# Polysketch attention and a multiplicative FFN on one core: a new global order of all steps behind the first batch's queries

## The chip, the cores and the metric

The kernel runs on one core of a Trainium2 chip. A core has five engines that run their own instruction streams side by side and wait for each other through semaphores: TensorE (PE, matrix products, with its weight loads shown apart as PEld), VectorE (DVE), ScalarE (ACT), GpSimd (POOL), and SyncE (SP), which here issues DMA transfers. Data lies in HBM, in SBUF (on-chip memory) and in PSUM (where matrix products land; eight banks).

The metric is the device time of one execution in microseconds (us). The kernel before has a median of 249.38 us over 3 runs (249.37 to 249.53).

## The reference

Four batches of four heads attend over 1088 positions of 32 dimensions; both queries and keys are turned into products of two 8-wide sketches, so no softmax and no score matrix is needed. The result, 4352 tokens of 128, goes through a gated feed-forward network (FFN) without a nonlinearity.

```python
def phi(x):
    a = np.einsum('rd,bhsd->bhsr', S1, x)      # r = 8
    b = np.einsum('rd,bhsd->bhsr', S2, x)
    return np.einsum('bhsi,bhsj->bhsij', a, b).reshape(*x.shape[:-1], r * r)
q_p, k_p = (phi(q), phi(k))
kv = np.einsum('bhsf,bhsd->bhfd', k_p, v)
z = np.sum(k_p, axis=2)
num = np.einsum('bhsf,bhfd->bhsd', q_p, kv)
den = np.einsum('bhsf,bhf->bhs', q_p, z)[..., None] + 1e-06
x = (num / den).transpose(0, 2, 1, 3).reshape(4352, 128)
a = x @ w1                                      # 128 x 1024
b = x @ w2
h = a * b @ w3                                  # 1024 x 1024
out = h @ w_out                                 # 1024 x 128
```

q, k and v are float32; the four weight matrices arrive as float64.

## The kernel before

All work is cut into named steps, a few instructions each. One long text, ORDER, lists every step once, in one global order. The kernel issues the steps in that order and chains each of the five engines' instructions to the one before it on the same engine, so ORDER fixes the sequence on every engine; what runs beside what follows from the waits. The compiler does not reorder anything.

```python
for name in ORDER.split():
    n = len(traced)
    steps.pop(name)()
```

Other tables at the top of the file belong to that order:

- SLOTS gives, for each kind of buffer, the buffer number of each allocation in the order in which they come. Kind b is the eight PSUM banks, raw the three landing buffers of the weights, x the three landing buffers that k, v and q share, and k_g, q_m, l, m and s are working buffers in SBUF. A step that takes over a buffer waits until its last readers are done.
- WARM[i] is the number of zero products in step warm{i} (line 255). They multiply a zero array and are read by nobody.
- POOL names the steps that run on GpSimd; without the name they run on VectorE. CPV names the copies that run on VectorE; without the name they run on ScalarE.
- Bulk loads on SP wait until the fourth load before them has landed (UNDER_WAY = 4). SP, too, goes strictly by ORDER.

The steps are named after what they work on. The prediction uses these:

- **s.** and **c.**: constants and sketch matrices. s.AR and the like belong to the preparation of the sketches.
- **w0 to w10**: the weights, float64 words made into float32. load (SP, lines 430, 433, 440), c and m (ScalarE, lines 263, 462, 484), j (VectorE, 466, 495), a0 and a1 (GpSimd, 470, 501). w0 and w1 belong to the matrices w1 and w2, number 2 is w_out, 3 to 10 are the rows of w3.
- **f0 to f7**: the fold of w3 and w_out into one matrix w3o: t is a transpose on VectorE (line 528), m eight products (534), o a copy (538). The FFN so needs no 1024 × 1024 product for the tokens.
- **k0 to k3**: the keys of a batch. load, zero (GpSimd clears the padding), max and lead and rest (the keys split into a leading and a remaining part, lines 214 and 651), gram (Gram products of the two, 659), G, T and N (small error-compensated sketch steps), ab, abt and kp (the features of the keys, 677), kv (769, 776), kvc, kqt and kq (the matrix that is multiplied by the queries' features).
- **q0, q1, q2, q3, q4, q6, qr**: queries (q4 and q6 are the last two whole batches, qr the rest tokens). tr, max, l2, l1, rm prepare; A0, C0 and C1 are the sketch products (1365, 1374); At, Ct, sm, st, sh, sl, sc make an error-compensated sketch (sl is line 1417); al, p01, p2, p12, dn, de, rc the denominator (1426 to 1454); bs, na to nn scale it (1459 to 1490); phi0 and phi1 the features (1509); pT0 and pT1 transpose them (1517); x multiplies them by kq (1527); xT0 to xT3 copy the result out of PSUM (1540, four copies each). After the queries' x come the tokens of the FFN.
- **g0 to g3**: the FFN of 512 tokens at a time, in eight slices of d_ff. For slice i, ia is x @ w1 (line 1799, a pair of products), ic its copy out of PSUM (1804), ib is x @ w2 (1809, a pair), im the elementwise product (1815), io the product by w3o (1835, a pair); oT transposes the output (1842), st stores it.
- **h4 and h6**: the FFN of the last two batches, 1024 tokens each, as a seven-product scheme after Strassen: a and b products of half arrays (1673), copies (1680), sums and elementwise products T and m (1685 to 1742), P products of half arrays (1759), k1 to k9 (1767 to 1785) and oT. **gr** is the FFN of the rest tokens (o at 1824).

Two queries matter most below. The chain for q4 and q6 runs sketch (TensorE), some thirty small steps on VectorE, ScalarE and GpSimd, phi, pT, then x on TensorE; between A0 and x TensorE works on g steps and folds.

Of the kernel before, what the change touches and what calls it, by code (L numbers as in the profile page):

```python
# [41 lines left out]
    "raw": "012012021020121",
    "s": "012345672403167520431760243517241",
    "x": "012012010221",
}

WARM = [27, 2, 3, 4, 4, 4, 1, 2, 1, 1, 2, 2, 1, 1]
# [18 lines left out]
    g0.1c g0.3c g2.1c g2.5c g2.6c g3.4c h4.0ad h4.0ae h4.0bd h4.1ac h4.2ad h4.k1 h6.2bd h6.3ae  # L66
    k0.kT1 k1.kvc k2.kT1 k2.kq k3.kT0 k3.kT1 k3.kq q0.xc0 q0.xc1
# [23 lines left out]
w2.load g0.6b g0.1a q1.pt1 k2.lead0 k2.rest0 q1.pc0 q1.pc1 q2.l2 q2.l1 q3.l1 g0.1b q1.x g0.5m q1.xT g0.3c g0.1c g0.1m  # L91
w9.m k1.Nr k2.gram0 k2.gram1 k2.gram2 k2.gram3 k2.gram4 k1.Nb k2.kT0 q3.rm q2.A0 q2.rm k1.kp0 k2.ab k2.abt q2.C0 q2.C1
g1.1a g1.1c v1.loadr k2.Gm q2.At q2.sm k2.Gt q2.Ct g1.5a w9.c k3.zero q2.st q3.A0 k2.Ga q3.C0 q3.C1 q3.Ct q2.sh k2.Gb
k3.load g1.7a v.s g1.7b g1.2a v1.load g1.7c q2.sl q2.sc q2.p01 q2.al q2.p2 k2.Gc q3.At g0.0b k1.kp1 q3.sm q3.st k1.kv0
q3.sh k2.T0 k1.kv2 k1.kv3 k1.kv1 k2.T1 k1.kvr k1.kvc kr1.kp g1.2c k2.Ta q2.p12 q2.dn q2.de k2.Tb g0.0m q2.rc g0.6m
q3.sl q3.sc q3.p01 w9.j g1.7m q1.restT q2.bs g1.6a g1.6c w2.c v2.zero q2.phi0 g1.2b k3.loadr g1.3a g1.3c g1.0a g1.5b
g1.3b k1.kqt warm12 w6.c w6.m g0.3b k1.kq g1.5c g1.4a k3.max g1.4c w5.load g1.1b v2.loadr kh3.load k0.Nr q2.load g1.3m
g1.5m g1.2m g1.0c q2.pT0 warm13 g1.0b k2.Tc q2.x g0.3m w9.a1 w5.m q2.xT0 k3.kT0 k2.N0 k2.N1 w5.c q3.al q3.p2 q3.p12
q3.dn w6.j g1.0m q3.de w7.load w2.m g1.4b w7.m w7.c w3.load w10.load w4.load v2.load w2.j k2.Na g1.4m k2.Nb q3.rc
k3.kT1 k3.lead0 q2.restT q3.bs g0.2b g2.6a g2.3a g2.1a g2.5a g2.4a g2.2a w5.j g1.1m g0.2m q3.phi0 k2.Nr g2.2b g2.0a  # L100
g2.3c g2.2c g2.4b g2.5c w3.c g1.6b k3.rest0 w9.a0 g2.4c w2.a0 g2.1c w2.a1 q4.tr k3.gram0 w6.a0 w5.a1 f6.t g2.2m
k3.gram1 k3.gram2 k3.gram3 k3.gram4 q3.pT0 f6.m g2.6b g2.6c g2.0c k3.Gm v.t g2.1b k3.Gt k3.Ga k3.Gb w7.j g2.4m q4.max
g2.7a g2.3b g1.6m q4.l2 w3.m k3.Gc w7.a0 g2.0b f6.o g2.3m w5.a0 w6.a1 v3.zero g2.1m q3.x q4.l1 k3.T0 k3.T1 g2.6m w3.j
g2.7c q4.rm g2.5b g2.5m q3.xT0 q3.load g2.7b g3.0a v3.load w8.load v3.loadr k3.Ta w4.m g3.0c g3.0b g3.0m g3.3a g3.1b
g3.1a g3.3c k3.Tb w3.a0 g3.1c g2.0m k2.kp1 q6.tr k3.Tc g2.7m w7.a1 f4.t g3.6a q3.restT g3.6c q4.A0 w3.a1 q6.max k3.ab
k3.N0 k3.abt k2.kp0 q4.C0 q4.C1 k3.N1 f4.m k3.kp1 g3.6b f0.t f3.t f4.o k3.kp0 f0.m q4.At q6.l2 g3.6m k2.kv0 k2.kv3
g3.1m w4.c w4.j k3.kv0 k3.kv1 k3.kv3 k3.kv2 k3.kvr q4.Ct q4.sm q6.l1 qr.max k3.kvc k2.kv1 k2.kv2 k2.kvr k2.kvc f3.m
w8.c f0.o f3.o w4.a1 w4.a0 g3.7a g3.7c g3.4b g2.0o k3.Na q4.st f1.t qr.l2 q6.rm q4.sh w10.m qr.l1 q4.sl q4.sc g3.5a
g3.4a g3.3b f1.m f1.o w10.c g3.4c g3.4m qr.rm k3.Nb q4.p01 w8.m q4.al k3.Nr k3.kqt g2.4o q6.A0 q6.C0 f2.t g3.3m q4.p2
v.3 q6.C1 k3.kq q6.At w8.j w8.a1 q6.Ct g2.6o g3.0o g3.4o qr.A0 qr.C0 qr.C1 qr.Ct q6.sm w10.j q6.st q6.sh q4.p12 w8.a0  # L110
g3.5b q6.sl w10.a1 q6.sc q4.dn qr.At g3.5c q4.de f5.t q4.rc g1.0o g1.1o q4.na q4.bs q4.nb f2.m q4.nm q4.nr qr.sm q6.al
q6.p01 q6.p2 g0.0o g0.1o q6.p12 f2.o g0.2o g0.6o k2.kqt g0.3o q4.ne g3.5m q4.nn q6.dn k2.kq f5.m f5.o g3.7b g3.2b
g1.6o g0.5o g0.4o w10.a0 qr.st f7.t f7.m g3.2a q4.phi0 q4.phi1 qr.sh qr.sl qr.sc f7.o q4.pT0 g3.2c q4.pT1 g2.5o g0.7o
# [36 lines left out]
def make_steps(ctx, tc, q, k, v, S1, S2, moe_w1, moe_w2, moe_w3, moe_w_out, out):  # L150
# [1784 lines left out]
```

## Time and profile before

| | before |
|---|---|
| median of 3 runs | 249.38 us (249.37 to 249.53) |
| the profiled execution | 248.89 us |
| its span on the core | 246.9 us |
| granted TensorE clock | 1.00 |
| read from HBM, written | 19.40 MB, 2.23 MB |

The span runs from the first to the last instruction that the profile shows. Busy time is given by engine; a row such as "L1835 PE MATMUL ps_o<-ab,w3o" names the line of the kernel, the engine, the operation, and what is written from what. Timeline rows begin with start and duration in us. The list of waits gives, for an engine, what it waited for: us in total, how often, the longest. "PE" in that list is time in which no product ran; "PEld" is the weight loads' own queue, whose waits are mostly hidden under running products. The chain of waits is followed back from the last instruction and here read in order of time.

### The profile page before, as it was taken

The numbers are of one execution on the slowest core, as the hardware profiler recorded it, in microseconds if no ns is written. First come the engines' busy times: TensorE is split into PE (matmuls) and PEld (weight loads), VectorE is DVE, ScalarE is ACT, GpSimd is POOL, SyncE is SP. The second block draws the span as 40 slices with busy tenths as digits, with TensorE's granted clock in tenths as the row PEclk, the third lists the DMA queues.
The fourth block names the chain that finished last, engine by engine and source line by source line (L and its number), as shares of the span: only waits on it lengthen the run. The fifth ranks groups of instructions, "written<-read, shape, count | busy, mean of one in ns | idle before, by whom it ended". The sixth has DMA issues, their size and how long they took to land.

```text
span 246.9 us, 6753 instructions
## 1 busy us (share of the span) xinstructions
PE 238.4 (97%) x2726; PEld 133.7 (54%) x2726; DVE 212.2 (86%) x426; ACT 121.8 (49%) x246; POOL 154.4 (63%) x198
## 2 busy tenths in 40 slices
PE   8999999999999999999999988999999999999994
PEld 6887464554445556856666434447653344463373
DVE  2787989988999889889899888588999699799892
ACT  3888965557865754674000195663562046430010
POOL 4475575608479489725579456998991927972111
PEclk9999999999999999999999999999999999999999
DMA  7969678275879776000000000340000004000034
GB/s 202 267 167 324 173 204 185 92 229 135 244 177 230 183 230 142 3 4 0 3 0 0 3 1 3 54 73 4 0 0 0 3 11 74 1 0 3 0 53 96
DMA packets 31934, 22.06 MB, mean 89 GB/s; under 512 B 21280, under 2 KB 26528, under 8 KB 31904
## 3 DMA queue, kind: packets, MB, share of 16 engines
q1 hardware_dynamic: 31360, 21.11, 34.3%
q10 hardware_dynamic: 544, 0.52, 0.6%
q8 instruction: 21, 0.34, 0.6%
q14 instruction: 9, 0.07, 0.1%
HBM read 19.40 MB, written 2.23 MB: 88 GB/s over the span
## 4 chain that ended last, share of the span: by engine, by line
PE 80%; DVE 15%; issue 2%; POOL 1%; ACT 0%; DVEq 0%
PE ps_X L1673 11%; PE ps_o L1759 10%; PE a_ps L1799 9%; PE b_ps L1809 9%; PE ps_o L1835 9%; PE ps_w3o L534 6%; PE ps_Y L1673 6%; PE idle_ps L255 4%; PE ps_Z L1673 3%; DVE ab L1815 3%; PE ps_g L659 2%; PE ps_ac L1374 2%; PE ps_kv L769 2%; PE ps_or L1824 2%; DVE pT L1517 1%
## 5 line engine op out<-in xcount | busy, mean ns | idle before, releaser
L1809 PE MATMUL b_ps<-xT,w 128*128 128x512 f32 (+1 forms) x80 | 36.4, 560 | 0.3 <-DVE ab L1815 0.2
L1673 PE MATMUL ps_X<-xd,wv 64*128 64x512 f32 x112 | 35.6, 595 | 0.0
L1799 PE MATMUL a_ps<-xT,w 128*128 128x512 f32 (+1 forms) x80 | 35.4, 558 | 0.0
L1804 ACT COPY ffa<-a_ps 128x512 f32<-128x512 f32 (+1 forms) x34 | 17.6, 536 | 30.4 <-PE a_ps L1799 30.3
L1680 ACT COPY hc<-ps_X 128x512 f32<-128x512 f32 x37 | 20.7, 589 | 21.2 <-PE ps_X L1673 12.9
L1835 PE MATMUL ps_o<-ab,w3o 128*128 128x512 f32 x64 | 29.4, 597 | 0.0
L1815 DVE TENSOR_TENSOR ab<-ffa,b_ps 128x512 f32<-128x512 f32 (+1 forms) x40 | 23.9, 619 | 3.2 <-PE b_ps L1809 2.5
L501 POOL TENSOR_TENSOR w3c<-w3c,cv_m 128x512 int32<-128x512 int32 x16 | 21.0, 1328 | 6.3 <-DVE w3c L495 6.3
L1799 PEld LDWEIGHTS a_ps<-xT,w 128*128 128x128 f32 x80 | 14.4, 190 | 14.6 <-issue 8.5
L1707 POOL TENSOR_TENSOR hc<-hc 128x512 f32<-128x512 f32 x15 | 19.7, 1327 | 2.9 <-DVE hc L1685 2.9
L1673 PEld LDWEIGHTS ps_X<-xd,wv 64*128 64x128 f32 x112 | 15.2, 186 | 10.4 <-issue 8.3
L1809 PEld LDWEIGHTS b_ps<-xT,w 128*128 128x128 f32 x80 | 14.0, 190 | 12.2 <-issue 7.7
L1673 PE MATMUL ps_Y<-xd,wv 64*128 64x512 f32 x48 | 19.2, 599 | 0.0
L1835 PEld LDWEIGHTS ps_o<-ab,w3o 128*128 128x128 f32 x64 | 11.7, 190 | 13.7 <-issue 13.2
L534 PEld LDWEIGHTS ps_w3o<-wo,w3T 128*128 128x128 f32 x128 | 15.3, 192 | 3.2 <-issue 2.5
L534 PE MATMUL ps_w3o<-wo,w3T 128*128 128x128 f32 x128 | 15.9, 277 | 0.6 <-DVE w3T L528 0.6
L1540 ACT COPY xd<-ps_x 64x256 f32<-64x256 f32 x32 | 11.7, 367 | 7.6 <-PE ps_x L1527 7.2
L538 ACT COPY w3o<-ps_w3o 128x128 f32<-128x128 f32 x8 | 2.0, 270 | 26.3 <-PE ps_w3o L534 26.3
L1759 PE MATMUL ps_o<-hc,w3o 128*64 128x512 f32 x32 | 14.7, 596 | 0.0
L1848 POOL TENSOR_TENSOR oT<-oT,nz 128x512 f32<-128x512 f32 x4 | 4.2, 1049 | 15.6 <-DVE oT L1842 14.4
L263 ACT ACTIVATE cv_c<-raw 128x1024 f32<-128x1024 f32 (+1 forms) x13 | 13.0, 1010 | 1.5 <-DMA raw<-in_moe_w_dram 1.5
L1509 POOL TENSOR_TENSOR ph<-s_al,s_bs 128x1024 f32<-128x1024 f32 x5 | 10.4, 2096 | 4.6 <-issue 4.5
(348 smaller groups left out, 604.4 us busy)
## 6 DMA issues: line engine op xcount, KB each, us to landing
raw<-in_moe_w_dram SPq DMA_DIRECT2D x32, 256.0 KB, 5.0
qh<-in_q_dram SPq DMA_DIRECT2D x4, 544.0 KB, 4.0
raw<-in_moe_w_dram SPq DMA_DIRECT2D x4, 512.0 KB, 6.0
out_dram<-oT SPq DMA_DIRECT2D x32, 64.0 KB, 1.9
k<-in_k_dram SPq DMA_DIRECT2D x3, 512.0 KB, 4.9
v<-in_v_dram SPq DMA_DIRECT2D x2, 512.0 KB, 6.8
kh<-in_k_dram SPq DMA_DIRECT2D x8, 128.0 KB, 2.4
raw<-in_moe_w_out_dram SPq DMA_DIRECT2D x4, 256.0 KB, 4.3
```

The costliest lines, as they stand in the source:

```text
L263: act.activation(dst, hi.bitcast(F32), ACT.Prelu, scale=2.0 ** -112, alpha=-2.0 ** 32)
L501: pool.tensor_tensor(d, d, x["m"][:, i * 512:(i + 1) * 512], ALU.add)
L534: pe.matmul(t["o"], w3T[ko][:, c], wo[:, c], start=c == 0, stop=c == NC - 1)
L1673: pe.matmul(x[bank], stat(j, u)[:, i * 128:(i + 1) * 128], rows(j, u), start=new, stop=True, tile_position=(u * 64, 0), skip_group_check=True)
L1680: cp(n(y))(x[k], x[bank])
L1707: on(f"h{g}.{i}m{k}").tensor_mul(both[0][k], both[0][k], both[1][k])
L1759: pe.matmul(acc_o[bank][half[0]:half[1]], w(i), x(i), start=n == 1, stop=n == (2 if j == 3 else 4), tile_position=(0, half[0]), skip_group ...
L1799: pe.matmul(x["a"][:, :w], w_of(0, c), xT[g][:, c0:c0 + w], start=True, stop=True)
L1804: cp(f"g{g}.{c}{su}c")(x["s"][:, :w], x["a"][:, :w])
L1809: pe.matmul(x["b"][:, :w], w_of(1, c), xT[g][:, c0:c0 + w], start=True, stop=True)
L1815: dve.tensor_mul(ab_sb[g, c][:, c0:c0 + w], x["s"][:, :w], x["b"][:, :w])
L1835: pe.matmul(o_ps[g], w3o[:, c], ab_sb[g, c], start=n == 1, stop=n == NC)
```

## The change

What each step computes is the same. The first 182 entries of ORDER (through the load of q1, at 26.5 us by the trace of before) are unchanged. Every step behind them stands in a new order, and the tables are made anew to go with it: SLOTS from there on, POOL, CPV and WARM.

Cut to its core:

```diff
@@ -27,44 +27,44 @@
 SLOTS = {
     "b": 
-        "012345670214657210671306537457462512346127340273051427362045726105341607575417607603461360"
...
+        "012345670214657210671306537457462512346127340273015406274170613214346210505012643106321431"
...
-    "raw": "012012021020121",
+    "raw": "010210120122121",
...
-    "x": "012012010221",
+    "x": "012012020121",
 }
 
-WARM = [27, 2, 3, 4, 4, 4, 1, 2, 1, 1, 2, 2, 1, 1]
+WARM = [27, 2, 3, 4, 4, 4, 1, 2, 1, 1, 2, 2]
...
 POOL = set("""
...
 CPV = set("""
-    g0.1c g0.3c g2.1c g2.5c g2.6c g3.4c h4.0ad h4.0ae h4.0bd h4.1ac h4.2ad h4.k1 h6.2bd h6.3ae
-    k0.kT1 k1.kvc k2.kT1 k2.kq k3.kT0 k3.kT1 k3.kq q0.xc0 q0.xc1
+    g0.0c g2.1c g3.1c gr.5c h4.0ad h4.0bd h4.2bd h4.3be h6.2ae h6.2bd k0.kT1 k1.kvc k2.kT1 k2.kq
+    k3.kT0 k3.kT1 k3.kq q0.xc0 q0.xc1 q4.xT0 q4.xT1 q4.xT2 q6.xT0
 """.split())
```

In POOL 33 steps come and 23 go. To GpSimd come h4.1T2 h4.1m22 h4.2T2 h4.3m11 h4.s1 h4.s3 h6.0T3 h6.0m11 h6.1T3 h6.2T1 h6.3T1 h6.3T4 k1.kp0 q1.bs q1.p2 q2.al q2.p01 q2.p2 q2.sc q2.sl q4.p01 q4.p12 q4.sl q6.bs q6.nn q6.p01 q6.p2 q6.phi0 qr.bs qr.p2 qr.phi0 qr.sc qr.sl. Back to VectorE go h4.0T3 h4.2m11 h4.2m12 h4.s2 h6.0T4 h6.1T1 h6.2T4 h6.2m12 h6.s1 k0.Nr k2.Nr k3.Nr k3.kp1 q2.bs q3.bs q3.p12 q3.sl q4.nn q4.phi0 q6.phi1 q6.sc q6.sl qr.p12.

The two steps dropped from WARM, warm12 and warm13, are one zero product each.

ORDER behind the shared part, at the places of which the prediction speaks (all else left out):

```diff
-w0.load k1.lead0 q0.xc0 q0.xc1 k0.kq w1.a1 k2.max q0.xt1 k1.ab q0.xT0 q0.xT1 g0.4a q1.load g0.5a q1.sm q1.Ct q1.st
-q1.sh k1.rest0 w0.m1 g0.4b g0.6a q1.sl q1.scy q1.sca g0.7a q1.p01 q1.al k1.abt k1.gram0 k1.gram1 k1.gram2 k1.gram3
-k1.gram4 q1.p2 w0.c1 w0.c0 g0.4c w0.j1 q3.tr g0.7b g0.5b kr1.abc q3.max q1.p12 k1.Gm q1.dn k1.Gt k1.Ga k1.Gb q1.de
-w9.load kh2.load q1.rc q1.bs w0.j0 g0.4m w0.a1 k1.Gc g0.5c g0.7c g0.7m k1.T0 k1.T1 g0.2a v1.zero q1.phi q3.l2 s.AR
-w0.m0 g0.0a g0.3a g0.2c k1.Ta k1.Tb s.RC k2.kT1 w0.a0 q1.pt0 k1.N0 q2.tr k1.Tc k1.N1 g0.6c q2.max k1.Na g0.0c w6.load
...
-k3.gram1 k3.gram2 k3.gram3 k3.gram4 q3.pT0 f6.m g2.6b g2.6c g2.0c k3.Gm v.t g2.1b k3.Gt k3.Ga k3.Gb w7.j g2.4m q4.max
...
-g0.oT g3.2m g3.3o g2.3o q4.x q4.xT2 q6.de qr.p01 q6.rc q4.xT0 q6.bs q6.nb q6.na g2.2o g2.7o qr.al q6.nm q6.nr q6.ne
-q6.nn v.1 q4.xT1 q6.phi0 q6.phi1 g1.4o o.S3 q4.xT3 g1.2o q6.pT0 g3.5o g3.7m q6.pT1 g1.3o q6.x qr.p2 q6.xT2 qr.p12
...
+w0.load k1.lead0 q0.xc0 q0.xc1 k0.kq w1.a1 k2.max q0.xt1 k1.ab q0.xT0 q0.xT1 g0.4a q1.load q1.sm q1.st q1.Ct w0.c1
+q1.sh k1.rest0 g0.5a g0.7a q1.sl q1.sca w0.j1 kh2.load q1.p01 g0.5c q1.al s.AR k2.kT1 q1.scy q1.p2 w0.c0 w0.j0 g0.6a
+q1.p12 k1.gram0 w0.m1 k1.gram1 k1.gram2 k1.gram3 k1.gram4 g0.4b g0.6c g0.4c k1.Gc k1.abt kh3.load q1.dn kr1.abc q1.de
+w0.m0 k1.Gm k1.Gt k1.Ga g0.5b w0.a1 s.RC q1.rc q1.bs q1.restT q3.tr q3.max g0.3a g0.7c g0.5m k1.Gb g0.2a g0.2c v1.zero
...
+k2.Ga q2.st q3.A0 q2.sh q3.C0 q3.C1 k1.kp0 k2.Gb g1.2a k1.kv0 k1.kv2 q2.sl q3.Ct q3.At w7.m q2.sc q2.p01 k1.kv3 k1.kv1
+k1.kvr q3.sm k2.T0 k2.T1 g1.3b w6.m k2.Ta k2.Tb w9.load w9.c g1.2b k1.kvc g1.3a q3.st q2.al g1.4a k2.Tc q2.p2 v3.zero
+g0.3b g1.3c q2.p12 q2.dn g1.2c w9.j q3.sh k3.loadr q2.de q2.rc q2.bs g1.7a q3.sl k3.kT1 g0.0b k3.max q3.sc q2.load
...
+w7.a0 q3.de g2.6a g2.4b w9.a0 w5.c g2.1c g2.5a g2.3c k2.Na g1.4b w2.c w7.a1 f6.t g2.4a g2.4c g2.5c q3.rc k3.Gm q3.bs
...
+w3.a1 g2.0a q3.pT0 g1.6b q4.l1 w4.c g2.2m f6.o w5.a1 g2.0b g2.6m g0.2m q3.x g1.6m g2.0c g2.0m k3.T0 k3.T1 q4.rm k3.ab
...
+g0.7o g0.5o g3.2a g3.2c k2.kqt q4.rc g0.0o g3.5m g3.7b q6.p12 v.t q4.bs q4.nb q4.nm q4.nr q4.ne q4.nn q4.phi0 q4.pT0
+q4.phi1 g3.2m k2.kq q6.dn q6.de q6.rc q6.bs q4.pT1 qr.al g0.4o q6.na q6.nb q6.nm q6.nr g3.4c q6.ne qr.p2 qr.p12 qr.dn
+g0.6o g3.7a qr.de g0.1o g3.1o g3.7c q4.x g0.2o q6.nn o.S1 g1.4o g0.oT g3.5o q6.phi0 g1.0o q4.xT2 g2.7o k3.kqt q4.xT0
+o.S3 q6.phi1 k3.kq g2.5o q4.xT3 g2.2o g3.2o g2.3o v.1 q6.pT0 qr.rc q6.pT1 g3.4b g3.4m g2.1o qr.bs g3.7m g2.0o q6.x
...
```

On SP the bulk loads come in a new order as well. Before, from w0 on: w0 q1 w9 kh2 w6 w2 v1.r k3 v1 w5 kh3 q2 w7 w3 w10 w4 v2 q3 v3 w8. After: w0 q1 kh2 kh3 w7 v1.r w6 v1 k3 w9 q2 w5 w2 w3 w4 v2.r v3 v2 q3 w10 w8. In the new numbering of the landing buffers (kind x) k3 takes the one that q1 had.

More of the change, by code (lines that the diff above doesn't have):

```diff
@@ L90 @@
-w0.m0 g0.0a g0.3a g0.2c k1.Ta k1.Tb s.RC k2.kT1 w0.a0 q1.pt0 k1.N0 q2.tr k1.Tc k1.N1 g0.6c q2.max k1.Na g0.0c w6.load
[L91 to L99, printed above, removed]
@@ L105 @@
[L105 to L113, printed above, removed]
-g0.oT g3.2m g3.3o g2.3o q4.x q4.xT2 q6.de qr.p01 q6.rc q4.xT0 q6.bs q6.nb q6.na g2.2o g2.7o qr.al q6.nm q6.nr q6.ne
```

108 lines of the change are left out of this document (61 added, 47 removed).

## The prediction

> **What bounds the kernel now.** I read the page's busy shares first, then the run cut into stretches, then the list of TensorE's waits, and last the chain of work that ended last.
>
> ```profile
> span 246.9 us, 6753 instructions
> ...
> PE 238.4 (97%) x2726; PEld 133.7 (54%) x2726; DVE 212.2 (86%) x426; ACT 121.8 (49%) x246; POOL 154.4 (63%) x198
> ```
>
> Busy us of each engine: TensorE (PE) is busy for 238.4 of a span of 246.9. The change keeps every product that computes something, so no order can take more than the other 8.5 us out of the span, and only if nothing has to wait.
>
> ```profile
> core 0: us, PE busy (x) PEld busy (x) DVE busy (x) ACT busy (x) POOL busy (x), PEclk, DMA share, GB/s
> 100.00:125.00 25.00, 25.00 (x384) 16.42 (x384) 22.35 (x47) 10.65 (x19) 13.08 (x12) 1.00 0.01 2
> 125.00:150.00 25.00, 23.52 (x186) 12.31 (x185) 22.93 (x40) 6.99 (x19) 15.52 (x15) 1.00 0.00 1
> 225.00:247.00 22.00, 18.24 (x98) 9.83 (x94) 16.20 (x29) 1.86 (x5) 3.85 (x4) 1.00 0.23 42
> ```
>
> The stretches: full from 100 to 125, 1.48 us short in the next one, 3.76 short in the last, where the final store runs after the last product. VectorE (DVE) is close behind TensorE in the middle (22.9 of 25), so an order that asks 2 us more of VectorE in front of some product shows at once. The granted clock (PEclk) is 1.00 throughout.
>
> ```profile
> engine line waited for: us in total, times, longest us
> PE ps_x L1527 <- DVE ab L1815: 1.1, 1, 1.1
> PE idle_ps L255 <- DVE zeros L229: 1.0, 1, 1.0
> PE ps_w3o L534 <- DVE w3T L528: 0.6, 1, 0.6
> PE ps_g L659 <- POOL kk L651: 0.6, 1, 0.6
> PE ps_x L1527 <- DVE pT L1517: 0.4, 1, 0.4
> PE ps_xs L1287 <- ACT xs L1280: 0.3, 1, 0.3
> ```
>
> TensorE's larger waits. The 1.0 at the start and the 0.3 (first batch) lie in the part of the order that both kernels share. What a new order can win is 1.1 + 0.4 = 1.5 at q6.x, 0.6 at a fold product (f6.m) and 0.6 at the Gram products k2.gram: 2.7 us. The chain of waits shows how the 1.5 arises (start, us, what):
>
> ```profile
> 137.11 1.73 PE ps_o L1835 x4
> 138.86 0.72 DVE oT L1842
> ...
> 143.57 2.87 DVE ph L1509
> 146.54 1.25 DVE pT L1517
> 147.78 0.57 DVE ab L1815
> 148.36 1.16 DVE pT L1517
> 149.56 1.36 PE ps_x L1527 x47
> ```
>
> From 138.86 to 149.56 the chain is on VectorE: feature product (ph), two transposes (pT), then the products q6.x. TensorE filled the time with half products at 1.73 / 4 = 0.43 us each and still came to q6.x 1.5 us early.
>
> **The change part by part.**
>
> *Two zero products dropped.*
>
> ```profile
> 1.00 5.54 PE idle_ps L255 x27
> ```
>
> 27 of them fill 5.54 us from 1.00 on, 0.205 each: −0.4. They stood just before steps whose inputs may have been what TensorE waited for, so the other bound is 0.
>
> *q6.x.* Between q6.A0 and q6.x nine pairs of half products come in (g3.5a, g2.7b, g3.4a, g3.7a, g3.1o, g3.2o, g3.4b, g2.1o, g2.0o) and three leave (g2.6o, g3.4o, g1.1o). A pair costs 2 × 0.43 = 0.86, so TensorE gets 6 × 0.86 = 5.2 us more cover. VectorE gets more to do there as well, above all two sets of x copies that ScalarE did. What follows q4.x decides. These are the prices:
>
> ```profile
> L1540 ACT COPY xd<-ps_x 64x256 f32<-64x256 f32 x32 | 11.7, 367 | 7.6 <-PE ps_x L1527 7.2
> L1804 ACT COPY ffa<-a_ps 128x512 f32<-128x512 f32 x26 | 14.9, 585 | 13.2 <-PE a_ps L1799 13.0
> L1804 DVE COPY ffa<-a_ps 128x512 f32<-128x512 f32 x6 | 4.0, 675 | 0.9 <-PE a_ps L1799 0.9
> 130.61 0.41 DVE L810 COPY kq<-ps_kq 128x256 f32<-128x256 f32 x1
> L677 DVE TENSOR_TENSOR kp<-kabt 128x1024 f32<-128x1024 f32 x1 | 1.2, 1219 | 0.0
> ```
>
> The same copy costs VectorE 675/585 = 1.15 times ScalarE's time, so the 0.367 becomes 0.42. Behind q4.x the new order on VectorE is: the wait for g0.2o (0.86), its oT (0.72), q4.xT2 and q4.xT0 (8 copies, 3.4), q6.phi1, k3.kq (0.41), pT (1.25), a small one (about 0.2), pT (1.16). For q6.phi1 I have 2.87 as it ran and 1.22 as a product of the same shape ran in another step. Sum: 9.2 to 10.9. TensorE has twelve pairs there, 10.3, and one small product: some 10.5. So the wait shrinks from 1.5 to between 0 and 0.4; I take 0.2, a gain of 1.3.
>
> *k2.gram and f6.m.*
>
> ```profile
> 41.40 2.65 POOL L651 TENSOR_TENSOR kk<-k,kk 128x1152 f32<-128x1152 f32 x1 [2.88 <-DVE kk L214]
> ```
>
> This is GpSimd's (POOL's) part of the keys, k2.rest0, which had itself waited 2.88 for VectorE's leading part, k2.lead0. By my list of the steps ahead of k2.lead0, VectorE has 0.3 less to do there in the new order (k1.Na, k1.Tb, g0.7m and two small query steps leave, g0.5m, g0.0c and two small ones come), and TensorE comes 0.8 later by the wait worked out next: 1.1 against the 0.6. The transpose f6.t stood right before f6.m; now eight pairs of products, 6.9 us, lie between the two, and VectorE's w5.j, g1.4m and others have moved behind it. Both waits go: −1.2. If each is replaced by a neighbour's wait, 0.
>
> *A new early wait.* g0.3a is brought forward past two other products to about 33.6, by TensorE's rate from the identical point on.
>
> ```profile
> 32.42 1.27 POOL L470 TENSOR_TENSOR w<-w,cv_m 128x512 int32<-128x512 int32 x1
> ```
>
> It reads the weight half that this step (w0.a1) finishes, which ended at 33.69. Now q1.p2 stands ahead of w0.a1 on GpSimd, and it needs q1.scy, which moved behind s.AR and k2.kT1 on VectorE. I count the end of w0.a1 at 34.1 to 34.7, so TensorE waits 0.5 to 1.1. With 0.3 of error on either side the bounds are 0.2 and 1.4; I take +0.8. Queued behind g0.3a are g0.2a and the sketch products k1.T, which nothing needs at once.
>
> *q4.x is pulled ahead.* Between q4.A0 and q4.x ten pairs and two smaller products (k3.ab, k3.kqt) leave TensorE and eight pairs come: 2.5 us less cover.
>
> ```profile
> 135.74 2.37 DVE L1517 STREAM_TRANSPOSE pT<-ph 128x1024 f32<-128x1024 f32 x2
> 140.47 1.50 PE L1527 MATMUL ps_x<-pT,kq 32*32 32x256 f32 x64
> ```
>
> Before, the transposes ended at 138.11 and TensorE came at 140.47: 2.4 to spare, which the lost cover uses up. VectorE takes q4.phi0 over from GpSimd (1.22 to 2.87) and gives steps such as q4.sl, qr.sl and f3.t away; by my list of the steps on both sides its work ahead of q4.pT1 changes by −0.1 to +1.6. So q4.x is on time at best and 1.7 late at worst; I take +0.5, the lower third, because TensorE's own small waits before that point give VectorE time. Next in line behind a late q4.x is g0.2o, for whose output VectorE waits.
>
> *Engines.* The sets move 33 steps to GpSimd and 23 away, so it gets ten more, at 154.4/198 = 0.78 each some 8 us: there is room (15.5 of 25 between 125 and 150). But work on GpSimd is not free for VectorE:
>
> ```profile
> 131.38 3.96 POOL L1509 TENSOR_TENSOR ph<-s_al,s_bs 128x1024 f32<-128x1024 f32 x2
> 133.57 1.93 DVE L1417 TENSOR_TENSOR s_hl<-ay_A,s_hl 128x128 f32<-128x128 f32 x1
> 135.53 0.29 DVE L1421 TENSOR_TENSOR s_hl<-s_hl,ay_C 128x128 f32<-128x128 f32 x1
> ```
>
> Two operations on VectorE of the same shape take 1.93 and 0.29; the long one began under GpSimd's long one and ended just after it. The Trainium skill ("SBUF — State Buffer", Who interferes with whom) gives the reason: a VectorE operation with two inputs in SBUF and a GpSimd operation that reads SBUF use one shared pair of ports, and one of them blocks. By that rule, which these rows bear out, the added GpSimd work speaks against the change.
>
> One such hit costs 1.93 − 0.29 = 1.64 us of VectorE. It costs time only where VectorE is what TensorE waits for, q4.x and q6.x; there it is the rival below and not in the sum.
>
> *Half-array products (last two batches) and tail.* The same products run in another interleaving. No wait of TensorE of 0.3 or more is listed there before, so there is nothing to win. In the last stretch VectorE's 16.2 stands beside TensorE's 18.2. I take 0, bounds −0.5 and +1.5.
>
> *New small waits elsewhere.* I add +0.4, about one each of the 0.4 and 0.3 that the list of before shows.
>
> Sum: −0.4 − 1.3 − 1.2 + 0.8 + 0.5 + 0.4 = −1.2 us. The profiled run took 248.89 with a span of 246.9, 2.0 around it. The span should become 245.7 and that run 247.7; the median of the runs shown, 249.38, is 0.49 above that run, which gives 248.2.
>
> **The rivals.**
>
> *q4.x becomes the long wait (slower).* If a GpSimd operation holds VectorE ahead of q4.pT1, q4.x is 1.7 + 1.64 = 3.3 late and not 0.5: sum +1.6, **251.0**. For it speaks that q4.sl, q4.sc, q4.p01, q4.p12 and q6.p01, q6.p2, q6.bs now run on GpSimd in just that stretch; against it that the two long feature products no longer run on GpSimd back to back. It decides as soon as q4.pT1 ends after TensorE's last product ahead of q4.x.
>
> *The gains are given back (same).* A step brought forward takes another's place: the 1.2 at k2.gram and f6.m comes back as waits of neighbours. **249.4**.
>
> *Weights late (slower).* The load of w9 is now queued on SP behind the load of k3, which waits for k3.zero on GpSimd, behind k2.rest0 (end 44.05).
>
> ```profile
> 50.37 2.60 SPq L440 DMA_DIRECT2D raw<-in_moe_w_dram  x4
> 68.09 4.16 SPq L440 DMA_DIRECT2D raw<-in_moe_w_dram  x5
> raw<-in_moe_w_dram SPq DMA_DIRECT2D x32, 256.0 KB, 5.0
> DMA to landing us min/median/max: 3.2/5.0/7.5
> L263 ACT ACTIVATE cv_c<-raw x13: 649/1155/1191, 14.3 to 113.1; 128x1024 f32<-128x1024 f32 x9, 128x512 f32<-128x512 f32 x4
> ```
>
> The four parts of a weight load took 2.6 to issue there, five took 4.16 at another place; one part lands in 5.0, at the worst in 7.5. From 44.05 that gives 51.7 at the usual prices and 55.7 at the worst, and some 0.7 more for the load of k3 ahead. ScalarE comes to the conversion w9.c at 51 to 52 by its list, so at the usual prices it waits about 1 us, which TensorE does not feel: the product g0.3b, which waits for k2.Tc on ScalarE behind w9.c, is due near 55.5 by TensorE's list. At the worst w9.c (1.16) ends at 57.6, k2.Tc 0.2 later, and TensorE stands for some 2.3 us: −1.2 + 2.3 = +1.1, **250.5**. It decides when the load lands after 54.
>
> *All early waits are absorbed (faster still).* Without the 0.8, the 0.5 and the 0.4 the sum is −2.9: **246.5**.
>
> **How the numbers follow.** What a measurement of this kernel can tell from no change is about 0.2%, 0.5 us. Forecast 248.2 (own range 247.2 to 248.9): 0.42. Faster still: 0.08. Given back: 0.15. q4.x late: 0.23. Weights late: 0.12. That makes faster 0.50, same 0.15, slower 0.35. The range from 246.4 to 251.2 takes in 246.5 and 251.0 with the rounding of their terms and leaves out some 0.15, most of it where the 1.5 of the tail adds to a late q4.x.
>
> **What would show it.** Right: TensorE's list of waits has no ps_x wait over 0.5, none of ps_w3o or ps_g, and one of 0.5 to 1.1 for w0.a1 (line 471 in the new numbering) near 33; the stretch from 125 to 150 is full. Wrong: a ps_x wait of over 2 us, ACT cv_c waiting for a weight transfer near 52 with TensorE idle behind it, or waits of TensorE within the half-array products, for which my sum has nothing.

## The result, and the profile after

| | before | after |
|---|---|---|
| median | 249.40 us (22 runs, 248.79 up) | 250.82 us (22 runs, 249.23 up) |
| ratio to before, 95% interval | | 1.0054 [1.0028, 1.008] |
| the profiled execution, its span | 248.89, 246.9 us | 252.91, 251.1 us |

The changed kernel is slower by about half a per cent, where 0.5% faster was forecast. Its times also spread more: apart from one outlier in each set, those of before lie between 248.8 and 250.5, those of after between 249.2 and 252.9. In a second set of 12 runs the unaltered changed kernel had a ratio of 1.0025 [0.9996, 1.0055], which can't be told from no change; four slow runs, over 1.5% above the fastest of that set, are left out of this ratio, and with them the medians are 250.63 and 249.29.

The page of the changed kernel, span and busy us of each engine:

```profile
span 251.1 us, 6763 instructions
...
PE 238.0 (95%) x2724; PEld 133.2 (53%) x2724; DVE 210.2 (84%) x428; ACT 118.0 (47%) x234; POOL 160.2 (64%) x208
```

TensorE has as much to do as before (238.0 against 238.4), so the 4.2 us of span that this execution is longer are all waiting. The stretches of the changed kernel say where:

```profile
25.00:50.00 25.00, 21.38 (x488) 11.83 (x494) 20.79 (x52) 17.46 (x34) 18.18 (x20) 1.00 0.85 207
50.00:75.00 25.00, 22.22 (x397) 11.30 (x379) 20.01 (x50) 13.76 (x23) 11.86 (x15) 1.00 0.62 150
...
125.00:150.00 25.00, 25.00 (x123) 11.07 (x122) 23.62 (x52) 5.61 (x11) 15.25 (x16) 1.00 0.00 1
```

From 125 to 150, where the prediction wanted 1.5 us back, TensorE is now full, but in part because everything comes later: q6.x now starts at 153, and what is left of its wait (0.7) lies in the next stretch. TensorE lost 3.6 and 2.8 us between 25 and 75 (before: 1.0 and 0.3). TensorE's waits in the changed kernel, the whole list over 0.2 us (line numbers are one higher than before):

```profile
PE ps_g L660 <- issue: 3.0, 2, 2.6
PE ps_kv L777 <- issue: 2.3, 1, 2.3
PE idle_ps L256 <- DVE zeros L230: 1.0, 1, 1.0
PE ps_N L913 <- issue: 0.8, 1, 0.8
PE ps_x L1528 <- DVE ab L1816: 0.7, 1, 0.7
PE ps_ac L1375 <- issue: 0.5, 1, 0.5
PE a_ps L1800 <- POOL w L471: 0.5, 1, 0.5
PE ps_xs L1288 <- ACT xs L1281: 0.3, 1, 0.3
```

Four rows have the releaser "issue": TensorE waited for nothing that the profile shows. Before, the list has no such row. Together they are 3.0 + 2.3 + 0.8 + 0.5 = 6.6 us. The waits for other engines, apart from the 1.0 at the start, fell from some 3.6 to 1.7. So between the engines the new order did what it was taken to do, and a wait of another kind, which stands in no term of the prediction, cost more than that.

**What TensorE waits for.** The rows of the timeline at the three longest of these waits show no semaphore:

```profile
48.20 0.22 PE L660 MATMUL ps_g<-k,kk 128*32 128x32 f32 x1 [2.62 <-issue]
58.77 0.30 PE L777 MATMUL ps_kv<-kpr,v 128*32 128x64 f32 x4 [2.28 <-issue]
98.72 0.19 PE L913 MATMUL ps_N<-T_p,P2b 32*32 32x8 f32 x1 [0.83 <-issue]
```

I counted TensorE's instructions (weight loads, products, semaphores) from the start to each of them. The five waits of over 0.3 us with this releaser fall on counts 1731, 1987, 2242, 2755 and 3267. Divided by 256, they leave 195, 195, 194, 195 and 195. And the page has a queue that moves instructions:

```profile
q8 instruction: 21, 0.34, 0.6%
```

That is 21 packets of 16,384 bytes, 256 instructions of 64 bytes each. TensorE's program is brought in block by block by transfers, and where a block is late TensorE stands at its border. The Trainium skill ("Runtime: NRT & Kernel Launch", Instruction fetch mechanics) describes such blocks of 16 KiB and calls the cost of a border mostly hidden. The size agrees with this trace, "mostly hidden" doesn't: a border cost up to 2.6 us here.

From the record of the transfers, per kernel: when TensorE crosses the border from which a block is asked for, when that block's packet starts and how long it takes, and the wait at the end of the 256 instructions between (us):

```
kernel    crossed   packet          TensorE waits
before      42.34   42.05 + 1.30    none
after       42.93   45.92 + 0.94    45.58 to 48.20
after       53.30   55.66 + 1.59    56.49 to 58.77
after       91.97   95.98 + 1.29    97.89 to 98.72
```

In the three rows with a wait TensorE goes on 1.3 to 1.5 us after the end of the packet. Each block comes 2.4 to 4.0 us after the crossing, plus its own 1 to 1.6, plus that. Meanwhile TensorE runs through 256 instructions. In the half-array products of the last two batches that takes 28.6 us (195.7 to 224.3 before); in the Gram products, which come at over 100 instructions a microsecond, less than 3.

Why is the packet late in one kernel and not in the other? Here is what SP issues in those microseconds, first before:

```profile
39.18 0.60 SPq L593 DMA_DIRECT2D v<-in_v_dram  x1
46.06 0.39 SPq L560 DMA_DIRECT2D k<-in_k_dram  x1
```

```profile
SPq L560 <- PE ps_g L659: 6.2, 1, 6.2
```

and in the changed kernel:

```profile
39.96 0.39 SPq L583 DMA_DIRECT2D v<-in_v_dram  x1
41.00 0.39 SPq L561 DMA_DIRECT2D k<-in_k_dram  x1
42.11 5.29 SPq L441 DMA_DIRECT2D raw<-in_moe_w_dram  x4
```

Before, the load of k3 waited 6.2 us for k2's buffer, until k2.gram was done, and SP issued nothing from 39.8 to 46.1. By the record of the transfers the 16 transfer engines were full until 42.1, when the packet went out, and all but idle from 43 to 47, under k2.gram. In the new numbering k3 takes q1's buffer, so its load goes out at 41.00, and w9's behind it; the transfer engines are full from 43 to 50. Two suspects then: the bulk loads in flight (theory A1), and the place of the border in the burst of small products (A2). Theory B is that neither matters and the order is worse in itself.

### The profile page after: what moved, and what is told of

Its sections match the earlier page's. It is cut to its first block, busy times and chain, and to the rows that moved or that the text cites. A ratio compares the mean times of both kernels' runs of the same rounds, so it can differ in the third digit from the quotient of the medians.

```text
span 251.1 us, 6763 instructions
## 1 busy us (share of the span) xinstructions
PE 238.0 (95%) x2724; PEld 133.2 (53%) x2724; DVE 210.2 (84%) x428; ACT 118.0 (47%) x234; POOL 160.2 (64%) x208
## 3 DMA queue, kind: packets, MB, share of 16 engines
q1 hardware_dynamic: 31360, 21.11, 34.5%
## 4 chain that ended last, share of the span: by engine, by line
PE 86%; DVE 7%; issue 4%; ACT 2%; POOL 0%; DVEq 0%; POOLq 0%; ACTq 0%
PE b_ps L1810 12%; PE ps_X L1674 12%; PE a_ps L1800 11%; PE ps_o L1760 10%; PE ps_o L1836 8%; PE ps_w3o L535 6%; PE ps_Y L1674 5%; PE idle_ps L256 4%; PE ps_Z L1674 3%; PE ps_g L660 2%; PE ps_ac L1375 2%; PE ps_x L1528 2%; PE ps_kv L770 2%; PE ps_or L1825 1%; DVE xd L1541 1%
## 5 line engine op out<-in xcount | busy, mean ns | idle before, releaser
L1674 PE MATMUL ps_X<-xd,wv 64*128 64x512 f32 x112 | 38.7, 593 | 0.0
L1800 PE MATMUL a_ps<-xT,w 128*128 128x512 f32 (+1 forms) x80 | 36.5, 562 | 0.5 <-POOL w L471 0.5
L1681 ACT COPY hc<-ps_X 128x512 f32<-128x512 f32 x38 | 21.3, 589 | 29.0 <-PE ps_X L1674 19.7
L1805 ACT COPY ffa<-a_ps 128x512 f32<-128x512 f32 (+1 forms) x36 | 18.6, 548 | 27.2 <-PE a_ps L1800 26.9
L502 POOL TENSOR_TENSOR w3c<-w3c,cv_m 128x512 int32<-128x512 int32 x16 | 20.1, 1275 | 10.9 <-ACT w3o L539 5.1
L1674 PEld LDWEIGHTS ps_X<-xd,wv 64*128 64x128 f32 x112 | 16.2, 187 | 12.4 <-issue 9.6
L1810 PEld LDWEIGHTS b_ps<-xT,w 128*128 128x128 f32 x80 | 14.2, 190 | 13.2 <-issue 9.0
L1686 DVE TENSOR_TENSOR hc<-hc,ps_X 128x512 f32<-128x512 f32 x16 | 10.8, 685 | 3.1 <-PE ps_X L1674 2.5
L1760 PE MATMUL ps_o<-tt,ws 128*64 128x512 f32 x32 | 13.1, 594 | 0.0
L1686 DVE TENSOR_TENSOR hc<-hc,ps_Z 128x512 f32<-128x512 f32 x16 | 10.6, 682 | 2.4 <-ACT hc L1681 1.2
L1541 ACT COPY xd<-ps_x 64x256 f32<-64x256 f32 x16 | 5.9, 366 | 14.2 <-PE ps_x L1528 14.0
```

What stands on the lines that cost most here:

```text
L502: pool.tensor_tensor(d, d, x["m"][:, i * 512:(i + 1) * 512], ALU.add)
L1674: pe.matmul(x[bank], stat(j, u)[:, i * 128:(i + 1) * 128], rows(j, u), start=new, stop=True, tile_position=(u * 64, 0), skip_group_check=True)
L1681: cp(n(y))(x[k], x[bank])
L1686: dve.tensor_add(x[k], x[k], x[bank])
L1760: pe.matmul(acc_o[bank][half[0]:half[1]], w(i), x(i), start=n == 1, stop=n == (2 if j == 3 else 4), tile_position=(0, half[0]), skip_group ...
L1800: pe.matmul(x["a"][:, :w], w_of(0, c), xT[g][:, c0:c0 + w], start=True, stop=True)
```

## The experiments

**Shifting the borders and nothing else.** The order of before, with more products in the first zero step, so that all borders fall earlier in the work. The products added are tiny (32 × 32), and some wide ones are taken out for them.

```diff
-WARM = [27, 2, 3, ...
+TINY = 71
+WARM = [20, 2, 3, ...
...
+            for _ in range(TINY if name == "warm0" else 0):
+                pe.matmul(t[:32, :32], zeros[:32, :32], zeros[:32, :32], start=True, stop=True)
```

> The kernel before with nothing moved, but with 64 TensorE products more ahead of everything (7 wide zero products taken out, 71 tiny ones put in, about the same time), so that the borders of the 256-instruction blocks in which TensorE's instructions are brought in fall 128 instructions earlier in the work. Theory A (TensorE stands where the next block of its instructions lands late): the kernel before, which has no such wait, gets them: waits put down to issue at new places, by my count of instructions and the landing times of the blocks some 5 to 8 us in all, time 254 to 257. Theory B (the losses of the changed kernel come from its order: waits between engines, clock): time within 1 us of before, or longer only by what the tiny products cost at the start (0 to 2 us), no issue waits over 0.3 us.

Measured: 259.42 us, ratio 1.0361 [1.0286, 1.0436]. The kernel before, in its own order, had become some 9 us longer by that ratio, more than theory A expected (254 to 257). Its waits for issue, of which its trace had none:

```profile
PE ps_c L1034 <- issue: 3.3, 1, 3.3
PE ps_w3o L538 <- issue: 1.1, 1, 1.1
PE ps_ac L1378 <- issue: 0.9, 1, 0.9
PE b_ps L1813 <- issue: 0.7, 1, 0.7
PE ps_kv L773 <- issue: 0.4, 1, 0.4
```

They stand on counts 962, 1475, 1987, 3010 and 3778: again 194 or 195 over a multiple of 256, at other places of the work than in the changed kernel. The sum is 6.4, as expected (5 to 8); the profiled span was 255.0, 8.1 over that of before. The longest, 3.3, ends at 24.8, in the part of the order that both kernels share. Right behind it, from 24.8 to 28.2, the trace's record of the granted clock shows half clock, where the kernel before has full clock from 6.0 us to its end; that is part of what the waits don't cover. The control shifts by a whole block (20 wide products out, 148 tiny ones in):

> Control for b_shift128: the kernel before with 128 TensorE products more at the start (20 wide zero products out, 148 tiny ones in; by the 0.027 us that a tiny one took in b_shift128 the same time within 0.1 us). 256 instructions more are exactly one block, so every border of a block falls where it fell before. Theory A: as before within 1 us (one more block to bring in at the start, no issue waits behind 25 us). Theory B (what made b_shift128 longer is the tiny products themselves or what they do to the clock): as long as b_shift128 or longer, 257 or more.

Measured: 251.45 us, ratio 1.0096 [1.0068, 1.0123], so theory A's "within 1 us" was missed, and theory B's 257 by far more. From 27 us to the end it is the kernel before, 2.7 us later: the waits at q6.x (1.1, 0.4), f6.m (0.6) and k2.gram (0.6) are as they were, and no new one follows. What is lost lies at the start, in these timeline rows and what follows them,

```profile
2.60 4.13 PE L259 MATMUL idle_ps<-zeros 32*32 32x32 bf16 x148
6.66 1.11 PE L689 MATMUL ps_kt<-ident,k 128*128 128x128 f32 x4
```

and in two waits for issue, at 16 and 22 us:

```profile
PE ps_kv L773 <- issue: 0.6, 1, 0.6
PE ps_g L663 <- issue: 0.3, 1, 0.3
```

The four ps_kt products took 0.66 in b_shift128, where the tiny ones filled 1.9 us; here, after 4.1 us of tiny ones, 1.11. The trace's record of the granted clock first shows the full clock at 9.9 us here, at 4.3 in b_shift128 and at 6.0 in the kernel before, which fits. So the tiny products aren't free, but they explain at most 2.7 us of the control, which has twice as many of them, and can't explain the 8 to 9 of the half block. A border in another place is enough to lose several us.

**Taking the bulk traffic away.** Both kernels with the loads of w_out and w3 cut to a quarter; the conversions read that quarter four times over, so three quarters of these weights are left out and the result is not that of the reference.

```diff
-                    sp.dma_start(raw[n][t * 32:(t + 1) * 32],
+                    sp.dma_start(raw[n][t * 32:(t + 1) * 32, :256],
...
-                                         ap=[[DF, 32], [32 * DF, 4], [1, 256]]))
+                                         ap=[[DF, 32], [32 * DF, 1], [1, 256]]))
...
-        words = lambda i: bview(raw[n].bitcast(I32)[:, i:], [[2, 1024]])
+        words = lambda i: bview(raw[n].bitcast(I32)[:, i:], [[0, 4], [2, 256]])
```

> The kernel before with each load of w_out and of the rows of w3 cut to a quarter (the converted weights are then made from that quarter four times over, so the fold works on wrong numbers; instruction counts and order of all engines as before). It is the partner of a_light. Theory A: it had no issue wait, so the time stays within 0.7 us of before. Theory B: the same.

> The changed kernel with the same cut of the loads to a quarter. Theory A1 (blocks of instructions late because of bulk transfers): issue waits behind 40 us fall from 6.6 us to under 3 us, the time falls by 1.5 to 4 us to about 247 to 249, and the order of the two turns round: a_light 0.5 to 2 us below b_light, which is what the new order saves in waits between engines (3.3 before, 1.7 after). Theory A2 (only the place of the borders): issue waits stay over 5 us, time as the changed kernel. Theory B (the order itself is worse in waits between engines): a_light stays 1 us or more above b_light.

Measured: before with light loads 249.09 us, ratio to before 0.9982 [0.9961, 1.0003]; the changed kernel with light loads **246.58 us, ratio 0.9885 [0.9855, 0.9916]**. TensorE's waits in the latter:

```profile
PE ps_g L661 <- issue: 0.9, 1, 0.9
PE ps_x L1529 <- DVE ab L1817: 0.7, 1, 0.7
PE ps_a L1112 <- issue: 0.4, 1, 0.4
```

The loads cost the kernel before 0.2 us and the changed one some 4. Less traffic also brings weights sooner, but the changed kernel's list had no wait for a weight to begin with; what fell are its waits for issue, from 6.6 to 1.3. Without most of the loads the new order is 2.5 us shorter than the old one: theory B falls. That 0.9 is left inside k2.gram though its block was sent 0.9 us after the crossing shows that the place counts too (A2 in part). In b_light that block's packet starts at 40.48, 2.1 us ahead of the crossing. There the last instructions ahead of the border are large products, and the last 64 take 3.2 us; in the changed kernel they are the tiny products of k1.N0 and k1.N1, which the new order put right before q1.x and the Gram products, and take 0.26 us. That a block is asked for some instructions ahead of the running product fits both; it was not tested by itself.

**Loads held back in the changed kernel.** A load waits for a product of TensorE, here v1 (and all loads behind it on SP) for k2.gram4:

```diff
+    HOLD, by_step = {'v1.load': 'k2.gram4'}, {}
...
+        by_step[name] = traced[n:]
+        if name in HOLD:
+            first = next(i for i in by_step[name] if i.engine == nc.sync.engine)
+            tc.add_manual_dep(first, by_step[HOLD[name]][-1].name, landed, reason="hold")
```

> The changed kernel with the load of v1, and all loads behind it on SP (k3, w9), held until the last k2.gram product. Theory A1: the 2.6 us issue wait in k2.gram falls to under 0.6 us, since no bulk transfer runs when that block is asked for; the waits behind it (k1.kv, 2.3 us) may stay or grow, since the loads now run there. Time 1 to 2.5 us below the changed kernel if nothing else is late. Theory A2 or B: the 2.6 stays; time same or longer by late loads.

Measured: 253.66 us, ratio to before 1.0168 [1.013, 1.0206].

```profile
PE ps_kv L777 <- issue: 3.3, 1, 3.3
PE ps_N L913 <- issue: 1.6, 1, 1.6
PE ps_g L660 <- issue: 1.2, 2, 1.0
PE ps_a L1111 <- issue: 0.5, 1, 0.5
```

With no bulk load under way the packet near 43 came 1.1 us after the crossing instead of 3.0, and the wait inside k2.gram fell from 2.6 to 1.0: in the direction of A1, though not to under 0.6. But the loads now ran under the k1.kv products, where the packet came 3.8 us after its crossing instead of 2.4, and the wait there grew to 3.3. The sum is 6.6 as before, and the time didn't fall: the hold moved the loss. With two smaller holds:

```diff
-    HOLD, by_step = {'v1.load': 'k2.gram4'}, {}
+    HOLD, by_step = {'w9.load': 'k2.gram4', 'w5.load': 'k1.kvr'}, {}
```

> The changed kernel with two loads held: that of w9 until the last k2.gram product (so not all loads, as in a_hold), that of w5 until the last k1.kv product. Theory A1: the block asked for near 43 and the one near 53 land some 1 us sooner each; the waits in k2.gram and at k1.kv (2.6 and 2.3) fall to 1 to 2 us each; time 1 to 2.5 us below the changed kernel, perhaps level with before, if w9 and w5 are still in time. Theory A2 or B: no change or longer.

Measured: 252.21 us, 1.0103 [1.0058, 1.0147]; issue waits 2.4 (k2.gram), 2.1 (k1.kv), 1.3 (N), 0.6 (at 20 us). The drop that was expected did not come: with w9 held, the loads already under way still kept the transfer engines full from 44 to 46.

**Fewer loads under way**, two and three, in the changed kernel.

```diff
-UNDER_WAY = 4
+UNDER_WAY = 2
```

> The changed kernel with at most two bulk loads under way instead of four. Theory A1: blocks land sooner while loads run (some 1 us less from border to landing between 40 and 100 us), issue waits fall from 6.6 to 2 to 4 us in all; weights later by a few us, which may add waits for them. Time 0 to 3 us below the changed kernel. Theory B: issue waits unchanged, time the same or longer.

> The changed kernel with at most three bulk loads under way instead of four. Theory A1: blocks of instructions land sooner while loads run, issue waits fall from 6.6 to 3 to 5 us; against that stand weights that come late, which with two under way cost 13.7 us of waits. Which of the two is larger with three is open: 248 to 256. Theory A2 or B: issue waits as in the changed kernel.

Measured with two: 268.81 us, 1.0768 [1.0711, 1.0826].

```profile
PE b_ps L1810 <- ACT T_p L909: 6.7, 1, 6.7
PE b_ps L1810 <- DVE N_g L218: 4.9, 1, 4.9
PE b_ps L1810 <- ACT kvc L800: 2.1, 1, 2.1
PE ps_g L660 <- issue: 1.3, 1, 1.3
...
PE ps_kv L777 <- issue: 0.4, 1, 0.4
```

The waits for issue fell to 1.7, as A1 says, but 13.7 us of waits for other engines came, above all where weights were late (ScalarE waited up to 11.5 us for one), and the granted clock fell to 0.86 from 50 to 75 and 0.85 from 100 to 125. The forecast of the time (0 to 3 below the changed kernel) was far off. With three: 250.74 us, 1.0027 [0.9993, 1.006], issue waits of 2.4 and 1.8 us; no difference from the changed kernel that can be told.

**Useless transfers under the Gram products of the kernel before.** Three of 512 KB, first released by k2.lead0, then (the diff) earlier by q2.tr, put on SP behind the load of w2.

```diff
+        if name == "w2.load":
+            at = by_step["q2.tr"][-1].name
+            for i in range(3):
+                nc.sync.dma_start(bass.AP(tensor=args[9].tensor, offset=i * 131072, ap=[[1024, 128], [256, 4], [1, 256]]),
+                                  bass.AP(tensor=args[1].tensor, offset=i * 131072, ap=[[1024, 128], [256, 4], [1, 256]]))
+                tc.add_manual_dep(traced[-1], at, landed, reason="extra")
```

> The kernel before with three useless transfers of 512 KB put on SP when k2.lead0 is done (about 41.3 us), into rows of the output that are written again later; order and instruction count of TensorE as before. Theory A1 (the block is late because bulk transfers are in flight when it is asked for): the block asked for near 42 lands 2 to 3 us later than before and TensorE stands 1.5 to 3 us inside the k2.gram products with the releaser issue; time +1.5 to +3. Theory A2 (only the place of the border in the burst matters, not the transfers) and theory B: no issue wait over 0.5 us at the Gram products, time within 0.7 us of before.

> As b_dummy, but the three useless transfers are released by q2.tr (about 40.1 us) and so run when the block for the second half of k2.gram is asked for, near 42; in b_dummy they came just too late for it. Theory A1: that block lands 1.5 to 3 us later than before and TensorE waits 1 to 2.5 us for issue inside k2.gram; time +1 to +2.5 over before. Theory A2 or B: no issue wait there, time within 0.7 us.

Measured: 250.99 us, 1.0072 [1.0038, 1.0107], and 251.13 us, 1.0028 [0.9986, 1.007]. In neither did TensorE wait for issue inside k2.gram. The packet had started at 42.43 and 41.42, in the first just as the useless transfers were issued, in the second while they ran, but 1.3 us ahead of the crossing all the same: the kernel before asks for that block early. The two miss their aim. They say that bulk transfers alone, at that place of the old order, make no wait for issue: A1 needs A2's badly placed border beside it. That the first is 0.7% longer neither theory expected; its profiled execution has a wait for issue of 1.2 us, but at 20.9 us, ahead of the useless transfers.

**A second trace of the changed kernel.**

> The changed kernel as it is, for a second trace. Theory A: its waits put down to issue, at the same places (k2.gram, k1.kv, N), add up to the span less 244.5 us (251.1 less 6.6 in the first trace), within 0.7 us, whatever the span is this time; the waits between engines are the same as in the first trace within 0.3 us. Theory B (something else makes the spread, the clock or the waits between engines): they do not follow the span.

Measured: profiled span 248.3 us.

```profile
PE ps_g L660 <- issue: 3.2, 2, 2.9
PE ps_x L1528 <- DVE ab L1816: 0.7, 1, 0.7
PE a_ps L1800 <- POOL w L471: 0.5, 1, 0.5
PE ps_kv L770 <- issue: 0.4, 1, 0.4
```

The waits for engines are those of the first trace. The waits at k1.kv and N are not there; two small ones are new, at 14.2 and 19.7. The block for k1.kv was sent 0.65 us after the crossing, not 2.35, in the same kernel: this time the transfer engines were under 10% busy from 53 to 56, while in the first trace the load issued at 53.10 filled them (68% from 54, full from 55). Issue waits of 3.6 leave 248.3 − 3.6 = 244.7, against 251.1 − 6.6 = 244.5 in the first trace. For these two traces the late blocks make the difference of 2.8 us. The clock does not: it is the shorter trace that has half clock, from 48.7 to 52.1, right behind its wait of 2.9. That late blocks make the spread of all 22 runs is likely by this, and not traced run by run; the clock takes part in it, since the 15 runs with a mean granted clock of 0.987 to 0.993 have a median of 251.6, the seven with 0.997 or more 249.8.

**The traffic and the packets, over all traces.** At the border of k2.gram in the changed order, the packet came 1.0 to 1.4 us after the crossing in the four traces in which the transfer engines were at most 81% busy in the microsecond ahead of it (a_hold, a_light, with two and with three under way), and 2.4 to 3.4 in the three in which they were full (both traces of the changed kernel, a_hold3). For all packets from 25 to 110 us in all 16 traces the median is 0.95 where the engines were under 10% busy and 2.25 where they were over 90%. Loads in flight are not the only reason: one block, asked for between 195 and 218 us with the transfer engines idle, came 4.4 us after its crossing in five traces of the changed order and 1.0 in two. All 33 waits for issue of over 0.3 us in these traces end at such a border, 1.3 to 1.7 us after the end of the block's packet.

**A version that beats both.** In its trace the kernel before has no late block (other traces of its order have one of 0.4 to 1.2 us between 19 and 26 us, ahead of all that is moved here), so its own waits are the ones to take: q6.x (1.5) behind three pairs of products, f6.m (0.6) behind g2.6b, with the two buffer numbers swapped.

```diff
-q3.pT0 f6.m g2.6b g2.6c
+q3.pT0 g2.6b f6.m g2.6c
...
-q6.pT1 g1.3o q6.x qr.p2 q6.xT2 qr.p12 qr.dn qr.de g3.1o g1.7o g3.6o g2.1o
+q6.pT1 g1.3o g3.1o g1.7o g3.6o q6.x qr.p2 q6.xT2 qr.p12 qr.dn qr.de g2.1o
```

> The kernel before with two moves of TensorE alone: q6.x three pairs of products later (behind g3.1o, g1.7o, g3.6o), and f6.m behind g2.6b. No load moves, and borders of blocks move by at most 12 instructions, none at a dense place. Theory A: the 1.5 us wait at q6.x and the 0.6 at f6.m go, nothing new comes: 247.0 to 247.8, below both kernels. Theory B (a wait taken away on TensorE comes back behind it, since VectorE is the bound there): within 0.7 us of before.

Measured: 250.12 us, 1.0021 [0.9993, 1.0048], as theory B has it. Both waits are gone, and a new one of 2.3, in two parts, stands at qr.x, for the PSUM banks that ScalarE's copies of q6.x free:

```profile
PE ps_x L1527 <- ACT xd L1540: 2.3, 2, 1.2
```

So the wait at q6.x had moved, not gone. With k2.lead0 ahead of k1.Na on top of that:

```diff
-g0.6c q2.max k1.Na g0.0c w6.load w2.load g0.6b g0.1a q1.pt1 k2.lead0 k2.rest0
+g0.6c q2.max k2.lead0 k1.Na g0.0c w6.load w2.load g0.6b g0.1a q1.pt1 k2.rest0
```

> b_best, and k2.lead0 ahead of k1.Na on VectorE, so that GpSimd's k2.rest0 starts about 0.5 us sooner. Theory A: the 0.6 us wait at k2.gram shrinks to 0.1 to 0.3; but the products of k2.gram then start nearer to the landing of the block that the second half of them needs (44.7 us against 45.5 when it is needed in the kernel before), so that up to 0.3 comes back as a wait for issue: 0 to 0.5 us below b_best. Theory B: no change against b_best.

Measured: 255.63 us, 1.0246 [1.0219, 1.0273], against both theories. k1.Na and what hangs on it came late, and TensorE waited 4.3 us for VectorE between 43 and 52:

```profile
PE ps_ac L1374 <- DVE q L1352: 1.9, 1, 1.9
PE ps_g L659 <- DVE ab L1815: 0.8, 1, 0.8
PE a_ps L1799 <- DVE kabt L745: 0.8, 1, 0.8
PE ps_ab L727 <- DVE kT L720: 0.8, 1, 0.8
```

Behind that the granted clock fell (third number from the right in the row of that stretch):

```profile
50.00:75.00 25.00, 24.08 (x321) 11.42 (x322) 20.38 (x60) 14.99 (x25) 8.15 (x11) 0.87 0.54 143
```

Last, b_best with the copy q6.xT1 on VectorE, behind qr.pT0, where VectorE was idle for 3.8 us:

```diff
-    k0.kT1 k1.kvc k2.kT1 k2.kq k3.kT0 k3.kT1 k3.kq q0.xc0 q0.xc1
+    k0.kT1 k1.kvc k2.kT1 k2.kq k3.kT0 k3.kT1 k3.kq q0.xc0 q0.xc1 q6.xT1
...
-h4.s1 h4.s3 q6.xT1 q6.ns g3.7o g3.2o qr.phi0 qr.pT0 g1.oT qr.x
+h4.s1 h4.s3 g3.7o g3.2o qr.phi0 qr.pT0 q6.xT1 q6.ns g1.oT qr.x
```

> b_best with one of the four copies behind q6.x, q6.xT1, on VectorE instead of ScalarE, behind qr.pT0. ScalarE's copies then end some 1.5 us earlier, and qr.x, which waited 2.3 us for them in b_best, waits 0.8 to 1.2; VectorE is idle for 3.8 us behind that place. Theory A: 247.7 to 248.5, 0.3 to 0.6% below the kernel before. Theory B (the wait moves on again): within 0.7 us of before.

Measured: **248.48 us, ratio 0.9962 [0.9942, 0.9983]**, 0.4% below the kernel before and within the forecast. The wait at qr.x is 1.1:

```profile
PE ps_x L1527 <- ACT xd L1540: 1.1, 1, 1.1
```

## Why the prediction was wrong, step by step

- **The missing term.** The sum (−1.2) had only waits between engines and late weights in it. It failed in "What bounds the kernel now": TensorE's list of waits was read as a list of inputs that come late, and nothing was asked about the supply of its instructions. The term it lacks is 3.6 us in one trace and 6.6 in the other.
- **The step that could have shown it.** "Weights late" has the load of k3 wait for k3.zero behind k2.rest0 (44.05), and w9's load behind it. But k3's load went out at 41.00 without waiting for k3.zero, which ran after it:

```profile
43.17 0.20 POOL L557 MEMSET k<- 64x128 f32 x1
```

So w9's load went out at 42.11 and both ran under the Gram products. The prediction weighed them only by when their data would land; no rival held that loads could keep TensorE's own instructions from coming. No run moved k3's load alone (a_hold moved v1, k3 and w9 together), so what its share is stays open.
- **The two zero products.** TensorE's busy time fell by the 0.4 forecast (238.4 to 238.0); what that did to the time no run shows.
- **q6.x.** Forecast left 0.2 of 1.5; 0.7 is left, outside the bounds of 0 to 0.4. Right in kind, the gain 0.8 and not 1.3.
- **k2.gram and f6.m.** Both waits for engines are gone, as forecast (−1.2).
- **The early wait for w0.a1.** Forecast 0.8 within 0.2 to 1.4; it is 0.5. w0.a1 ended at 34.5, within the 34.1 to 34.7 that was counted.
- **q4.x and new small waits.** Forecast 0.5 and 0.4; the list has none of 0.3 or more for either. The rival of a long wait at q4.x did not come. GpSimd's added work (5.8 us in all) shows in TensorE's waits only in the 0.5 for w0.a1, which now stands behind q1.p2.
- **The half-array products and the tail.** No wait over 0.2 there, as taken.
- **Weights late.** No wait of TensorE for a late weight. The rival's time (250.5) is near the measured one for another reason; that is luck.

Counted by the two pairs that share a condition, the order is worth −2.5 us (246.58 against 249.09, light loads), twice the forecast gain; with the loads as they are, the late blocks take that back and about 1.4 more (250.82 against 249.40). That the late blocks are TensorE's instructions, and that border and loads decide, is shown by b_shift128, its control, the light pair and the 33 waits at borders. How far ahead TensorE asks for a block, on which shared resource the packet waits, and why some packets come late without traffic, was not tested. An alignment of the changed kernel's borders that suits it was not searched for.

## What to carry to other kernels

A kernel with many small products can have a second supply to plan: instructions, 256 to a block here. Look for waits of TensorE with the releaser "issue", count instructions to them, and keep bulk loads and borders away from the densest bursts; a new order, or a few zero products more or less, moves the borders. A wait removed ahead of an engine that still has copies to make can come back at the next product that needs their banks, as 2.3 us did in b_best; with one copy on another engine 1.1 was left.

## What the runs showed that was not expected

- 128 instructions more in the first microseconds (71 tiny products for 7 wide ones), with no other edit, made the kernel before some 9 us longer; 256 more cost 2.4 us, in the trace all of it before 27 us.
- A block could be used 1.3 to 1.7 us after its packet had ended. At the borders named above its packet started from 2.1 us ahead of the crossing to 4.4 us after it, as a rule later with bulk loads in flight.
- After 4.1 us of 32 × 32 products, four 128 × 128 products took 1.11 us, where they took 0.66 after 1.9 us of such; the full clock was on record from 9.9 us there, from 4.3 here.
- The granted clock fell to a half for 3.4 us right behind a wait of 2.9 us for instructions (the second trace of the changed kernel) and of 3.3 (b_shift128) and 2.4 (three loads under way), and for 6.8 us among the waits of b_best2 (0.87 from 50 to 75). Behind the 2.6 and 2.3 us of the first trace of the changed kernel it stayed at 1.00. So the length of a wait alone doesn't decide; what does was not tested.
